# One transfer instead of four for a turned tile, the order made by the fetch, and sums of fetched tiles no longer forced

## The chip, the cores and the metric

The kernel runs on one core of a Trainium2 chip. A core has a matrix engine (TensorE, PE in the profile, its weight loads PEld), a vector engine (VectorE, DVE), a scalar engine (ScalarE, ACT), a general engine (GpSimd, POOL) and a sync engine (SyncE, SP) whose queue issues most transfers; 16 DMA engines carry the transfers. The metric is the time of one execution on the device in microseconds (us).

## The reference

Attention with a block mask over 4 batches of 8 heads, 768 positions and 64 columns; its output, laid out as 768 x 512 for each batch, goes through a Fourier mix and a two-layer channel network. All of it is float32.

```python
scores = scale * np.matmul(q, k.transpose(0, 1, 3, 2))        # (4, 8, 768, 768)
scores = np.where(mask, scores, -1000000000.0)                # blocks of 32 x 32
attn = np.exp(scores - max) ; attn = attn / (sum + 1e-09)
x = np.matmul(attn, v) -> (4, 768, 512)
mixed = np.real(fft(fft(x, axis=1), axis=2))
u = x + mixed
un = (u - mean(u)) / np.sqrt(var(u) + 1e-06)                  # over the 512 columns
out = u + np.maximum(un @ w_ch1, 0.0) @ w_ch2                 # 512 -> 2048 -> 512
```

## The kernel before

**Attention** goes in slots. A slot is two units; a unit is one chunk of 128 keys against 384 queries, for a pair of heads. There are 24 slots to a batch (6 for each of 4 pairs of heads), 96 in all. A slot multiplies the scores on PE (line 578), takes their exponential on ACT and multiplies the values in on PE (line 652), one or two slots later. The mask is applied in one of two ways. Early on PE adds it to the scores in two more products of a unit (line 588), ACT's exponential (line 598) writes the result, and sums of the weights are gathered by DVE (line 633) or POOL (line 638). Once `masks["by_pe"]` is false, ACT writes the exponential back (line 606) and DVE multiplies it with the mask (line 608). Pairs of heads from the sixth on are fetched in blocks of 32 x 32 (`load_blocks`, line 230): four transfers of 96 KB each for a tile of queries or keys (`qb`, `kb`), in pieces of 32 numbers, 128 bytes.

**The mixer** of a batch runs beside the attention of the next one. First its steps on x: folding, products with cosine and sine tables, normalising. Each step makes three tiles of 128 positions x 512 columns for each of two halves of the positions, `un`. The channel network wants them turned, columns on the partitions. For the last batch PE turns them. For batches 0, 1 and 2, which this change is about, the path is:

- `un_blocks` (line 1010): DVE turns each 32 x 32 block of a tile in place.
- Also in `un_blocks` (line 1013): SP writes the tile to a scratch tile `far` in memory. Four transfers, one for each 32 partitions, put every block where it belongs: `far` of a half is 32 x 16 x 384, and a piece is 32 numbers, 128 bytes.
- `un_back` (line 1022): SP fetches both halves into `unT`, four transfers of 32 partitions each for a half, 192 KB each. Every piece read is a row of 384 numbers.
- `right` (line 1053): four DVE sums of blocks of the fetched `unT`, which the first products of the channel network need (Strassen's scheme with seven products instead of eight, `quad`, line 1091). `left` (lines 1066, 1067, 1073) makes the same kind of sum from the weights.
- `quad` and `channels` (line 1147) then multiply; DVE adds the product to x (line 1150) and SP stores it (line 1158). Only when x of batch b - 2 is stored may `place` (ACT, line 676) write attention results of batch b into the same room.

**The order** is written out when the kernel is built, by a planner with a clock `when` for each engine and a cost for each step. Two lists hold the mixer's work: `apart`, the steps up to and including `right`, and `late`, the products. `gap` takes steps of `apart` where they fit beside PE's work; a step of kind "b", which all four sums are, has to wait in `gap` until the planner's clock has reached `state["back"]`, the time at which it expects the fetch to be in. The planner sets that in `un_back`, `BACK` after its own clock. Behind the four sums stands the step `go`: it makes `late` available and sets `masks["by_pe"]` to false. At the end of a slot of the third and fourth batch, where `late` is empty and few steps of `apart` are left, a loop takes up to four of them whatever the clock says:

```python
for _ in range(4 if phase > 1 and not late and len(apart) < 6 * T else 0):
    if apart and not late:
        do_apart()
```

The engines follow the order of the build: an instruction that waits holds up everything behind it on its engine, and so does a transfer in the queue of SP.

Of the kernel before, what the change touches and what calls it, by code (L numbers as in the profile page):

```python
# [11 lines left out]
FP32 = mybir.dt.float32  # L12
# [10 lines left out]
def _words(ap, n):  # L23

    return bass.DRamTensorHandle(ap.tensor.name, (2 * n,), I32)
# [74 lines left out]
def kernel(  # L100
# [14 lines left out]
    nc = tc.nc  # L115

    B, H, S, D = q.shape
    DM = H * D
    FF = w_ch1.shape[1]
    P = 128  # L120
    C = S // P
    BLK = 32
    NB = S // BLK
    NR = sampled_blocks.shape[1]
    HS = S // 2
# [4 lines left out]
    T = C // 2  # L130
# [54 lines left out]
    far_p = ctx.enter_context(tc.tile_pool(name="far_p", bufs=1, space=bass.MemoryType.DRAM))  # L185
# [7 lines left out]
    when = {"PE": 0.0, "ACT": 0.0, "DVE": 0.0, "POOL": 0.0}  # L193
# [106 lines left out]
    def bit(n):  # L300
# [5 lines left out]
                      in_=bass.AP(tensor=_words(sampled_blocks, NB * NR), offset=0,  # L306
                                  ap=[[0, NB], [1, 2 * NB * NR]]))
# [670 lines left out]
    def mixer(b, xA, xB):  # L978


        uns, unT = {}, {}
# [21 lines left out]
        lines = {}  # L1003

        def un_blocks(half, m):

            un = uns.pop((half, m))
            if half not in lines:
                lines[half] = far_p.tile([BLK, DM // BLK, HS], FP32, tag=f"un{half}", name="far")
            nc.vector.transpose(out=un, in_=un)  # L1010
            for g in range(P // BLK):
                n = m * P + g * BLK
                nc.sync.dma_start(out=lines[half][:, :, n:n + BLK],
                                  in_=un[BLK * g:BLK * g + BLK, :].rearrange(
                                      "j (t i) -> j t i", i=BLK))

        def un_back():

            for half in range(2):
                unT[half] = tr_p.tile([P, ND, T * P], FP32, tag="tr", name="unT")  # L1020
                for a in range(P // BLK):
                    nc.sync.dma_start(out=unT[half][BLK * a:BLK * a + BLK, :, :],
                                      in_=lines[half].rearrange(
                                          "j (k a) n -> a j k n", a=P // BLK)[a])
            state["back"] = max(when["PE"], state["ready"]) + BACK

        t, s = {}, {}
        K1, K2 = slice(0, ND // 2), slice(ND // 2, ND)
# [169 lines left out]
        def outputs(r, m, after):  # L1198
# [60 lines left out]
            if r == 1:  # L1259
# [5 lines left out]
              for h in range(2)]  # L1265

        ft = [[("d", lambda h=h, m=m: un_blocks(h, m), 0.0, 0.0, 0.7) for m in range(T)]
              for h in range(2)]

# [9 lines left out]
        if not last:  # L1279
            before = first + [pq[1], ar[0][1], ar[1][1], sp[0][1],  # L1280
                              pq[2], wh[0][1], ft[0][1], ar[0][2], ar[1][2], sp[0][2],
                              pq[0], wh[0][2], ft[0][2], ar[0][0], ar[1][0], sp[0][0],
                              sp[1][1], wh[0][0], ft[0][0], sp[1][2], wh[1][1], ft[1][1],
                              sp[1][0], wh[1][2], ft[1][2], wh[1][0], ft[1][0]]
            after = ([("-", un_back, 0.0, 0.0, 0.0)] + le +
                     [("b", lambda i=i: right(i, 0, 1, 2), 0.0, 0.0, 1.0) for i in (1, 2, 3, 4)])
# [5 lines left out]
        for r in range(0 if last else NF // 4):  # L1292
# [9 lines left out]
    MOST, LEAST = 9.6, 2.5  # L1302
    COVER = 100.0
    AHEAD = 2.2
    BACK = 9.0
    ALONE = 3.0
    LEAVES = 9.0
    SP = UP // SLOT
# [2 lines left out]
    short, apart, late, due = deque(), deque(), deque(), deque()  # L1311
    asked = set()
    needed = set()
    state = {"paired": False, "total": None, "w": 0, "got": 0, "owed": 0.0, "ready": 0.0,
             "back": 0.0}
# [9 lines left out]
    def do_apart():  # L1325
        kind, fn, pe, act, dve, _ = apart.popleft()
        if kind[0] in "dwb":
            dve += behind(kind)
            state["ready"] = busy("DVE", dve, {"w": rstd_at[0] if rstd_at else 0.0,
                                               "b": state["back"]}.get(kind, state["ready"])) + HOP  # L1330
            fn()
            return
        done = state["ready"]
        if kind != "-":
            at = bank(kind[0])
            done = busy("PE", pe, done) + HOP
        fn()
        if act:
            done = busy("ACT", act, done) + HOP
        if dve:  # L1340
            done = busy("DVE", dve, done) + HOP
        if kind != "-":
            give(at, done - HOP)
        state["ready"] = done
# [74 lines left out]
    def slot(sl):  # L1419
        phase, r = divmod(sl, SB)  # L1420
        n, s = divmod(sl, SP)
# [48 lines left out]
        if s >= (5 if reuse else 3) and (n, 0) in oT_at and once(n):  # L1470
            b, j = pairs[n]
# [13 lines left out]
        if sl < B * SB and n % NP == 1 and s == 1:  # L1485
            b = pairs[n - 1][0]
# [35 lines left out]
            gap(rest())  # L1522

        for _ in range(4 if phase > 1 and not late and len(apart) < 6 * T else 0):
            if apart and not late:
                do_apart()

        must = (3, 5) if paired else (2, 5)
# [5 lines left out]
        while short and (not more or soon) and (  # L1534
                s in must or len(short) > 1 or phase == 0 or soon or sl == B * SB):
            ready = [i for i in short if max(i[1], min(free[i[0]])) <= when["PE"] + 0.1]
# [36 lines left out]
    for sl in range(B * SB + 1):  # L1573
        slot(sl)
        if sl == B * SB - 4:
            flag = highest()
        if sl == B * SB - 2:
            over = nc.values_load(flag[0:1, 0:1], min_val=0, max_val=1)
# [107 lines left out]
```

## Time and profile before

| what | value |
|---|---|
| median of 3 runs | 1062.29 us (1061.61 to 1062.72) |
| the profiled execution, its own time | 1060.62 us |
| its span in the trace | 1058.8 us, granted clock 0.991 |
| PE busy | 1022.0 us, 97% |
| DVE, ACT, POOL busy | 677.8, 356.5, 241.6 us |
| transfers of `far` (72 of 64 KB) and of `unT` (24 of 192 KB) | SP queue |

The profile names engines as above; SPq, PEq and so on are the queues in front of them. A row of a timeline gives the start and the length in us, the engine, the line in the kernel, the operation, what it writes and reads, how many instructions are merged and, in brackets, how long the engine had been idle before and what ended that. A wait for several things is put down to the one that came last by the profile's reckoning; transfers on the same queue can be mistaken for each other there. A row of stretches gives for each engine the busy time (and the instructions), then the granted clock of PE, the mean busy share of the 16 DMA engines, and GB/s.

### The profile page before, as it was taken

To read this page: it belongs to the slowest core of one execution; us is meant where nothing else is said; L and a number is where in the kernel's file an instruction comes from. 1 tells how busy PE (TensorE), PEld (TensorE's weight loads), DVE (VectorE), ACT (ScalarE), POOL (GpSimd) and SP (SyncE) were. 2 spreads that over 40 slices of the span, in tenths; PEclk is the share of its full clock that TensorE was granted. 3 is DMA by queue.
4 is the path that set the end of the run, shared out by engine and by line. 5 is a ranking of instruction groups with operands and counts; after the bars stand their busy time and mean duration, and the time that the engine had idled before them with its cause. 6 is when DMAs were issued, how large, how long until landed. Compare 5 with 4: busy or idle time off the path is not lost.

```text
span 1058.8 us, 12480 instructions
## 1 busy us (share of the span) xinstructions
PE 1022.0 (97%) x4334; PEld 529.7 (50%) x4334; DVE 677.8 (64%) x1236; ACT 356.5 (34%) x718; POOL 241.6 (23%) x272
## 2 busy tenths in 40 slices
PE   8999999987999999999999999899999999999996
PEld 4333345433465554444444654344444654578575
DVE  6898795968754845564578466665457364674663
ACT  6988755553120112342441210253220211210210
POOL 1000183554200100554553001255520001000000
PEclk9999999998999999999999999999999999999999
DMA  7757422381000124222230003621000001000001
GB/s 214 230 170 225 108 46 46 50 147 28 1 0 11 20 44 96 57 38 44 41 56 1 1 11 60 134 43 27 12 10 5 1 1 37 24 1 1 1 16 47
DMA packets 162017, 55.72 MB, mean 53 GB/s; under 512 B 146572, under 2 KB 155034, under 8 KB 161946
## 3 DMA queue, kind: packets, MB, share of 16 engines
q1 hardware_dynamic: 160694, 54.11, 22.7%
q10 hardware_dynamic: 1220, 0.72, 0.3%
q8 instruction: 36, 0.59, 0.2%
q14 instruction: 35, 0.29, 0.1%
q0 software_dynamic: 32, 0.01, 0.0%
HBM read 41.44 MB, written 11.01 MB: 50 GB/s over the span
## 4 chain that ended last, share of the span: by engine, by line
PE 82%; DVE 6%; DMA 3%; ACT 3%; SPq 2%; issue 2%; POOL 0%; ACTq 0%; DVEq 0%
PE y L1147 22%; PE z L1091 15%; PE s L578 11%; PE o L652 9%; PE yp L1091 7%; PE yy L1212 7%; PE xp L1091 4%; PE zp L856 2%; PE sp L719 1%; DVE t L1053 1%; ACT e L598 1%; DMA kb<-in_k_dram 1%; PE s L588 1%; DMA out_dram<-x 1%; PE sp L733 1%
## 5 line engine op out<-in xcount | busy, mean ns | idle before, releaser
L638 POOL TENSOR_TENSOR acc<-acc,e 128x384 f32<-128x384 f32 x162 | 164.6, 1052 | 97.4 <-DVE e L608 81.1
L578 PE MATMUL s<-qT,kT 64*128 64x384 f32 x768 | 156.5, 523 | 20.4 <-DVE e L608 13.1
L652 PE MATMUL o<-e,vr 128*64 128x384 f32 x768 | 142.4, 498 | 0.0
L1147 PE MATMUL y<-w_sb,hB 128*128 128x512 f32 x288 | 128.6, 597 | 0.3 <-DVE x L1150 0.3
L1147 PE MATMUL y<-w_sb,hA 128*128 128x512 f32 x288 | 127.9, 595 | 0.0
L1150 DVE TENSOR_TENSOR x<-y,x 128x512 f32<-128x512 f32 x72 | 49.7, 691 | 111.7 <-PE y L1147 111.6
L608 DVE TENSOR_TENSOR e<-s,mask 128x768 f32<-128x768 f32 x92 | 83.8, 951 | 58.1 <-ACT s L606 49.9
L578 PEld LDWEIGHTS s<-qT,kT 64*128 64x128 f32 x768 | 64.4, 187 | 100.1 <-DVE e L608 28.0
L638 POOL TENSOR_TENSOR acc<-e 128x384 f32<-128x384 f32 x44 | 48.5, 1123 | 257.3 <-PE sp L733 127.2
L606 ACT ACTIVATE s<-s 128x768 f32<-128x768 f32 x92 | 70.0, 792 | 92.6 <-PE s L578 92.4
L1091 PE MATMUL z<-unT,t 128*128 128x384 f32 x256 | 93.2, 487 | 0.7 <-DVE hA L1096 0.7
L598 ACT ACTIVATE e<-s 128x768 f32<-128x768 f32 x100 | 76.0, 810 | 48.6 <-PE s L588 29.6
L1147 PEld LDWEIGHTS y<-w_sb,hB 128*128 128x128 f32 x288 | 53.6, 191 | 67.2 <-issue 65.7
L1147 PEld LDWEIGHTS y<-w_sb,hA 128*128 128x128 f32 x288 | 53.7, 190 | 63.7 <-issue 60.2
L652 PEld LDWEIGHTS o<-e,vr 128*64 128x64 f32 x768 | 48.1, 137 | 71.5 <-issue 68.0
L1096 DVE TENSOR_TENSOR hA<-z,hA 128x384 f32<-128x384 f32 x64 | 35.7, 557 | 68.5 <-PE z L1091 68.5
L1100 ACT ACTIVATE hA<-hA 128x384 f32<-128x384 f32 x64 | 33.4, 523 | 123.8 <-DVE hA L1096 123.8
L1091 PEld LDWEIGHTS z<-unT,t 128*128 128x128 f32 x256 | 48.5, 190 | 35.4 <-DVE hA L1096 2.0
L1100 ACT ACTIVATE hB<-hB 128x384 f32<-128x384 f32 x64 | 33.5, 523 | 86.2 <-DVE hB L1096 83.8
L1111 ACT COPY hA<-xp 128x384 f32<-128x384 f32 x32 | 15.3, 478 | 128.6 <-PE xp L1091 128.6
L1091 PE MATMUL yp<-unT,w_sb 128*128 128x384 f32 x128 | 46.7, 487 | 0.8 <-ACT hA L1111 0.6
L1091 PE MATMUL xp<-unT,w_sb 128*128 128x384 f32 x128 | 47.2, 492 | 0.0
(208 smaller groups left out, 1364.2 us busy)
## 6 DMA issues: line engine op xcount, KB each, us to landing
wraw<-in_moe_w_ch_dram SPq DMA_DIRECT2D x32, 512.0 KB
vr<-in_v_dram SPq DMA_DIRECT2D x30, 192.0 KB
far<-un SPq DMA_DIRECT2D x72, 64.0 KB
unT<-far SPq DMA_DIRECT2D x24, 192.0 KB
qb<-in_q_dram SPq DMA_DIRECT2D x44, 96.0 KB
kb<-in_k_dram SPq DMA_DIRECT2D x44, 96.0 KB
x<-oT SPq DMA_DIRECT2D x192, 12.0 KB
out_dram<-x SPq DMA_DIRECT2D x11, 252.0 KB
```

Of the source, the lines that this page charges most:

```text
L578: nc.tensor.matmul(s[:, i, 0:HS], kT[rows, c * P:(c + 1) * P], qT[rows, queries], start=True, stop=u not in by_pe)
L598: nc.scalar.activation(out=e, in_=s[:, :, 0:HS], func=ACT.Exp, scale=scale)
L606: nc.scalar.activation(out=s[:, :, 0:HS], in_=s[:, :, 0:HS], func=ACT.Exp, scale=scale)
L608: nc.vector.tensor_tensor(out=e, in0=s[:, :, 0:HS], in1=m.broadcast_to([P, 2, HS]), op=ALU.mult)
L638: nc.gpsimd.tensor_add(out=acc[:, i, :], in0=start[:, i, :], in1=e[:, i, :])
L652: nc.tensor.matmul(o[D * i:D * i + D, :], vt[:, i, c, :], e[:, i, :], start=(c == 0), stop=(c == C - 1))
L1091: nc.tensor.matmul(to, a[:, k, :], c[:, k, :], start=(k == 0), stop=(k == ND // 2 - 1))
L1096: tt(out=to, in0=ps, in1=a, op=ALU.add)
L1100: nc.scalar.activation(out=h, in_=h, func=ACT.Relu)
L1147: nc.tensor.matmul(y, hs[0, half][:, l, m * P:(m + 1) * P], w2_sb[:, 4 * r + l, :], start=(l == 0), stop=(l == 3))
L1150: nc.vector.tensor_tensor(out=x[:, m, :], in0=y, in1=x[:, m, :], op=ALU.add)
L1212: nc.tensor.matmul(ps, a[:, k, :], c[k // 2][:, k % 2, :] if isinstance(c, list) else c[:, k, :], start=(k == 0), stop=(k == 3))
```

## The change

It has three parts. The scratch tile `far` takes a turned tile as it is, 128 partitions of 512 numbers, in one transfer of 256 KB where there were four of 64 KB. The order is now made by the fetch: its eight transfers still fill 32 partitions each with 192 KB, but every piece they read is 32 numbers, 128 bytes, 1536 pieces to a transfer where there were 128. In the planner, `BACK` goes from 9.0 to 13.0 for the first batch and 12.0 for the others, and the loop at the end of a slot no longer takes a sum of fetched tiles before the planner's clock has come to `state["back"]`.

```diff
             if half not in lines:
-                lines[half] = far_p.tile([BLK, DM // BLK, HS], FP32, tag=f"un{half}", name="far")
+                lines[half] = far_p.tile([T, P, DM], FP32, tag=f"un{half}", name="far")
             nc.vector.transpose(out=un, in_=un)
-            for g in range(P // BLK):
-                n = m * P + g * BLK
-                nc.sync.dma_start(out=lines[half][:, :, n:n + BLK],
-                                  in_=un[BLK * g:BLK * g + BLK, :].rearrange(
-                                      "j (t i) -> j t i", i=BLK))
+            nc.sync.dma_start(out=lines[half][m], in_=un)
 
         def un_back():
             for half in range(2):
                 unT[half] = tr_p.tile([P, ND, T * P], FP32, tag="tr", name="unT")
+                of = lines[half].rearrange("m (g j) (k a i) -> a j k (m g) i",
+                                           j=BLK, a=P // BLK, i=BLK)
                 for a in range(P // BLK):
-                    nc.sync.dma_start(out=unT[half][BLK * a:BLK * a + BLK, :, :],
-                                      in_=lines[half].rearrange(
-                                          "j (k a) n -> a j k n", a=P // BLK)[a])
-            state["back"] = max(when["PE"], state["ready"]) + BACK
+                    nc.sync.dma_start(
+                        out=unT[half][BLK * a:BLK * a + BLK].rearrange(
+                            "j k (g i) -> j k g i", i=BLK),
+                        in_=of[a])
+            state["back"] = max(when["PE"], state["ready"]) + BACK[b > 0]
...
-    BACK = 9.0
+    BACK = 13.0, 12.0
...
         for _ in range(4 if phase > 1 and not late and len(apart) < 6 * T else 0):
-            if apart and not late:
+            if apart and not late and (apart[0][0] != "b" or
+                                       state["back"] < max(when["DVE"], when["PE"]) + 0.2):
                 do_apart()
```

## The prediction

> **What bounds the kernel now.** I read the head of the page first, then PE's waits, then the timelines of the three places where `unT` is fetched.
>
> ```profile
> span 1058.8 us, 12480 instructions
> PE 1022.0 (97%) x4334; PEld 529.7 (50%) x4334; DVE 677.8 (64%) x1236; ACT 356.5 (34%) x718; POOL 241.6 (23%) x272
> PE 82%; DVE 6%; DMA 3%; ACT 3%; SPq 2%; issue 2%; POOL 0%; ACTq 0%; DVEq 0%
> ```
>
> PE bounds it. Only 36.8 us of the span (1058.8 - 1022.0) are free of a product, so a change that adds and removes no product can gain only there, or where PE ran at a lower clock. PE's waits, in total, times and longest:
>
> ```profile
> PE s L578 <- DVE e L608: 13.1, 4, 8.1
> PE s L578 <- ACT e L598: 6.9, 12, 1.9
> ```
>
> The largest is a score product waiting for DVE's masking, and most of that is one wait of 8.1 us. The timeline at the first fetch shows it:
>
> ```profile
> 222.52 0.68 DVE L1010 STREAM_TRANSPOSE un<-un 128x512 f32<-128x512 f32 x1
> 223.78 2.69 SPq L1013 DMA_DIRECT2D far<-un  x4
> 226.16 0.95 DVE L633 TENSOR_TENSOR acc<-acc,e 128x768 f32<-128x768 f32 x1
> 226.32 1.56 PE L578 MATMUL s<-qT,kT 64*128 64x384 f32 x8
> 226.51 5.19 SPq L1022 DMA_DIRECT2D unT<-far  x8
> 229.58 1.56 PE L578 MATMUL s<-qT,kT 64*128 64x384 f32 x8
> 234.24 1.56 PE L578 MATMUL s<-qT,kT 64*128 64x384 f32 x8
> 236.96 1.11 DVE L1053 TENSOR_TENSOR t<-unT 128x768 f32<-128x768 f32 x1 [9.85 <-DMA kb<-in_k_dram]
> 241.33 1.74 DVE L1053 TENSOR_TENSOR t<-unT,t 128x768 f32<-128x768 f32 x1
> 244.33 1.80 DVE L608 TENSOR_TENSOR e<-s,mask 128x768 f32<-128x768 f32 x2
> 245.32 2.93 PE L578 MATMUL s<-qT,kT 64*128 64x384 f32 x8 [8.08 <-DVE e L608]
> ```
>
> The four forced sums stand on DVE right behind the row of 226.16. DVE stands still 9.85 us until the fetch is in (the release is booked on `kb`, which follows on the same queue), sums until 243, and only then reaches the masking that PE waits for. PE loses 8.08 us, and the first eight products after it take 2.93 us where the same take 1.56.
>
> At the second fetch nothing is lost:
>
> ```profile
> 394.15 8.93 SPq L1022 DMA_DIRECT2D unT<-far  x8
> 404.00:414.00 10.00, 10.00 (x24) 4.35 (x24) 5.63 (x7) 0.00 (x0) 0.00 (x0) 1.00 0.47 110
> 408.08 0.95 DVE L1053 TENSOR_TENSOR t<-unT 128x768 f32<-128x768 f32 x1
> 410.90 0.69 DVE L1150 TENSOR_TENSOR x<-y,x 128x512 f32<-128x512 f32 x1
> ```
>
> The sums start without a wait and PE is busy 10.00 of 10 us. At the third, two things go wrong one after the other:
>
> ```profile
> 649.41 5.02 SPq L1013 DMA_DIRECT2D far<-un  x4
> 653.53 0.69 DVE L1150 TENSOR_TENSOR x<-y,x 128x512 f32<-128x512 f32 x1 [0.75 <-PE y L1147]
> 656.34 2.63 SPq L1013 DMA_DIRECT2D far<-un  x4
> 659.07 1.21 SPq L1158 DMA_DIRECT2D out_dram<-x  x2
> 662.31 0.48 ACT L676 COPY x<-xt 128x384 f32<-128x384 f32 x1 [17.97 <-DMA out_dram<-x]
> 664.54 2.79 PE L578 MATMUL s<-qT,kT 64*128 64x384 f32 x8 [3.06 <-DVE e L608]
> 667.26 4.12 PE L1147 MATMUL y<-w_sb,hB 128*128 128x512 f32 x8
> 676.03 1.82 DVE L1053 TENSOR_TENSOR t<-unT 128x768 f32<-128x768 f32 x1 [3.93 <-DMA kb<-in_k_dram]
> 680.78 0.68 DVE L1150 TENSOR_TENSOR x<-y,x 128x512 f32<-128x512 f32 x1
> ```
>
> The last x of half A is ready at 654.2 (653.53 + 0.69), but its store is issued at 659.07, behind eight writes of `far`. ACT waits for the store until 662.31; its exponential, DVE's masking and PE's scores follow, and PE loses 3.06 us. Then the sums wait 3.93 us on DVE, and the last sum into x stands behind three of them (680.78).
>
> **The change, part by part.** *One write instead of four.* The counts and sizes, what two kinds of transfer get out of the DMA engines, and what products of line 1147 take undisturbed:
>
> ```profile
> L1013 SPq DMA_DIRECT2D far<-un x72: 549/627/2036, 193.0 to 665.1; - x72
> unT<-far SPq DMA_DIRECT2D x24, 192.0 KB
> qb<-in_q_dram SPq DMA_DIRECT2D x44, 96.0 KB
> 230.00:231.00 1.00, 1.00 (x10) 0.51 (x8) 0.00 (x0) 0.87 (x3) 1.00 (x2) 1.00 1.08 218
> 247.00:248.00 1.00, 1.00 (x4) 0.10 (x2) 0.09 (x1) 0.80 (x1) 1.00 (x2) 0.50 0.99 160
> 331.06 10.30 PE y L1147 x24
> ```
>
> 54 issues of 0.627 us fall away, 34 us of SP's queue over the kernel. SP bounds nothing by itself, so this counts in one place. At 649 to 659 six of the eight issues ahead of the store go: 3.8 us (6 x 0.627), and the store moves from 659.07 to about 655.3. That is more than PE's 3.06 us, so I take them as gone, and with them the slow products behind: 1.2 us (2.79 - 1.56) and 0.7 us (4.12 less 3.4, a third of 10.30). Sum at the third fetch 5.0 us. The bounds are 0, if the write of 256 KB keeps the store back instead, and 5.0.
>
> The Trainium skill, DMA: Bandwidth & Descriptors, section Issuing engines are not separate DMA queues, says that a sequencer's issue time is usually small beside the transfer. By that, joining issues would save next to nothing and the 5.0 us would not come. The rows are against it here: eight issues of `far` stand in the queue between 649.41 and 659.07, and the store behind them. I go by the rows, and keep the page's case as a rival below.
>
> *The fetch makes the order.* Still 24 fetches of 192 KB, but in pieces of 128 bytes. No row shows that fetch. Its nearest row is the load of `qb` at 247, the same direction and the same pieces: 160 GB/s with the engines full (0.99). The old fetch of long rows ran at 218 (row of 230). Eight transfers are 1573 KB: 7.2 us before, 9.8 us now, 2.6 us more. Lower bound 7.2 us, upper bound 15.0 us, if reading such pieces back from scratch goes only as fast as the queue wrote them (64 KB in 0.627 us, 105 GB/s). I take 9.8. In return the last write before the fetch holds SP 0.6 us instead of 2.69, and the transpose before it ends at 223.2, so the fetch starts at about 224.0 instead of 226.51, 2.5 us sooner. The two nearly cancel: it lands at about 237, as now. The next load of `kb` stands behind it on the queue as it does now.
>
> The Trainium skill, DMA: Bandwidth & Descriptors, section Specifications, gives 512 bytes as the least transfer for full rate. The rule speaks against the change, and the two rows agree with it in kind (160 against 218 GB/s). Where it would lead if the loss were far greater is the third rival.
>
> *Sums not forced, expected later.* At the first fetch the planner now expects the data 13 us after the last transposed tile, on the trace's time at 223.2 + 13 = 236.2. The loop no longer takes the sums at the end of the slot of 226 (229.6), nor can they go at the end of the next (234.2). They go in the slot that begins at 234.24, two slots later. By then the data is all but there: 237 less 236.2 leaves DVE a wait of up to 1 us instead of 9.85. Behind the sums on DVE is queued the masking of the slot after. Four sums at the present 1.1 to 1.7 us end at 242 to 243, and the scores of that slot's successor have to wait for a masking behind them. PE is dry there from about 240.8 (two slots of 3.26 us, 226.32 to 229.58, after 234.24), so I leave 2 us of wait. What goes: 8.08 us and 1.4 us (2.93 - 1.56) of slow products, 9.5 in all. What comes: the 2 us, and two more slots masked by PE, because `go` stands behind the sums.
>
> ```profile
> 224.62 0.33 PE s L588 x4
> ```
>
> Those are 0.33 us a slot in the chain, 0.7 us. Sum at the first fetch: 9.5 - 2.0 - 0.7 = 6.8 us gained; bounds 3 (the sums end at 246, as long as PE's dry spell lasts) and 9.
>
> At the second fetch the planner's 12 us put the sums one product of 3.4 us later, behind the row of 410.90. Work that hides it: PE's products until 414. The second half of the fetch takes 1.3 us longer (half of 2.6) and has 3.4 us to do so. Zero; if the cover were gone, up to 3 us lost. At the third the sums likewise fall behind the last product of batch 1, so the last sum into x goes ahead of them and its store starts up to 5 us sooner than behind 680.78, and the next use of that room with it. PE's leftovers there:
>
> ```profile
> 676.00:680.00 4.00, 2.97 (x9) 1.31 (x8) 3.93 (x3) 0.48 (x1) 2.71 (x3) 1.00 0.40 93
> 692.00:696.00 4.00, 3.32 (x18) 1.26 (x20) 2.95 (x4) 3.21 (x10) 3.23 (x4) 1.00 0.33 53
> ```
>
> 1.0 and 0.7 us are idle. I count 1.0 us of the 1.7 as gained; the bounds are -2 (the first products of batch 2 wait for sums that start later) and +1.7.
>
> Sum: 6.8 + 5.0 + 0 + 1.0 = 12.8 us. For waits that the new order brings and that I can't place I take 1.5 us off: 11.3. The profiled execution took 1060.62 us (span 1058.8 and 1.8 around it), 0.16% under the median of 1062.29, so it would come to 1049.3, and the median to 1051.0.
>
> **The rivals.**
> *Only the first fetch gains.* The store at 659 is held by the data of the writes, not by their issue, or another wait takes its place. For it: the second issue row, 5.02 us for four, is longer than four times 0.627. Against: the chain goes through SP's issues there. Gain 6.8 - 1.5, about 5.3 us: 1057.0.
>
> *The sums stall again.* The fetch takes the 15.0 us of the upper bound and lands 5.2 us after my 237; the sums hold DVE until 248, and the first fetch gains nothing. The third keeps its 5.0 us, as it has time: 1057.3 by the median. For it: the scratch rows are read in scattered pieces; against: `qb` is too, at 160 GB/s.
>
> *The fetch is far slower, and it ends slower than before.* If the pieces come back at 65 GB/s, a fetch takes 24.2 us and lands at 251. The sums then end at 257, the scores two slots on start at 258.5 instead of about 249.7 (245.32 + 2.93 + 1.4): 9 us lost. At the second fetch the second half alone takes 12.1 us from about 402 and the sums wait 3; at the third they start at 685, 9 us later than now, with the first products of batch 2 behind. Together 21 us lost less the 5.0 us of the store: 1078. It decides from about 85 GB/s downwards, half of what `qb` shows. The skill's 512-byte rule, which points this way, would have to bite twice as hard as in the row.
>
> *The change does nothing that counts*: the loop finds the sums due at the same slot after all, and the gain by the store is eaten by the longer fetch: 1062. Against: 13 us after 223.2 is past the end of both slots.
>
> **How the numbers follow.** Forecast 1051.0: 0.58. Only the first fetch: 0.14. Stall again: 0.10. Far slower, or a new order that costs more than it saves: 0.12. Nothing: 0.06, half of it within 0.2%, which is about what a measurement of this kernel can tell from no change. Faster 0.84, same 0.03, slower 0.13. The forecast's own range is 1045 to 1055: all bounds good (9 + 5.0 + 1.7, 1046.6, and no new waits) to a first fetch at its lower bound of 3 us (1054.8). The range of 1045 to 1062 takes in the next two rivals and no change at all, and leaves 0.05 below and 0.13 above.
>
> **What would show it.** Right: no idle of DVE over 2 us ahead of the first sum at any fetch; the sums at the first fetch after 236; PE's longest wait on the masking under 3 us; in the slot of 234 the row of line 588 still there; ACT's copy at 662 gone to about 658 with PE's 3.06 us; 18 writes of `far`; a fetch in about 10 us. Wrong: a bracket of some microseconds on the first sum again; a store of x still landing after 661; the engines full at well under 160 GB/s while `unT` comes in; PE's clock low in a new place.

## The result, and the profile after

| | us |
|---|---|
| kernel before, median of 15 runs beside it | 1061.33 (1059.89 to 1064.09) |
| changed kernel, median of 15 runs | 1058.52 (1054.26 to 1059.52) |
| ratio | 0.9966, interval 0.9957 to 0.9975 |
| predicted, by the 1062.29 of then | 1051.0 |

The change makes the kernel faster, by 2.8 us where 11.3 were predicted. The profiled execution took 1059.17 us, 0.65 over the median. It is 1.45 us under the profiled execution of the kernel before (1060.62), where the medians are 2.8 apart: the two profiles show only half of the difference. Its page begins:

```profile
span 1057.5 us, 12421 instructions
...
PE 1022.8 (97%) x4338; PEld 530.7 (50%) x4338; DVE 675.3 (64%) x1235; ACT 356.2 (34%) x718; POOL 240.2 (23%) x270
```

PE's waits (total, times, longest):

```profile
PE s L578 <- DVE e L608: 6.5, 3, 3.7
...
PE z L1090 <- DVE e L608: 3.4, 1, 3.4
...
PE z L1090 <- DVE hA L1095: 2.0, 1, 2.0
PE z L1090 <- DVE t L1052: 1.6, 1, 1.6
```

The wait of 8.1 us on the masking is gone. In its place stand 3.7 and 2.0 us on the masking (the first row) and the 3.4, 2.0 and 1.6 us of the others. (Line numbers of the changed kernel are one or two lower than before: the write is line 1011, the fetch 1020, the sums 1052, the quad 1090, the product of `channels` 1146, the add to x 1149, the store 1157.)

The best ruler is the start of a quad's first product, the row `xp<-unT,w_sb`, since each quad follows a fetch and its sums. Between two such marks the order of PE's work is nearly the same in both kernels:

| mark | before, starts at | after, starts at | gained since the mark above | foreseen |
|---|---|---|---|---|
| last quad ahead of the second fetch | 391.37 | 386.73 | +4.6 (first fetch) | +6.8 |
| first quad of batch 1 | 428.22 | 427.48 | -3.9 (second fetch) | 0 |
| last quad of batch 1 | 634.00 | 633.25 | 0.0 | 0 |
| first quad of batch 2 | 675.63 | 670.10 | +4.8 (the store) | +5.0 |
| second quad of batch 2 | 700.41 | 698.75 | -3.9 (after the third fetch) | +1.0 |
| end of the span | 1058.8 | 1057.5 | -0.4 | 0 |

Beside these the prediction took 1.5 us off for waits that it couldn't place. Nearly all that the first fetch and the store gain is given back at two places, a few microseconds further on.

Of the first +4.6, only 2.9 come at the fetch itself. By the slot of 206 us (206.48 before, 206.24 after) the changed kernel is 0.2 ahead; 1.5 more come between there and the fetch, where a wait of PE of the kernel before is gone:

```profile
223.01 1.62 PE L578 MATMUL s<-qT,kT 64*128 64x384 f32 x8 [1.23 <-ACT e L598]
```

This wait stands in the three kernels with the old writes and in none of the ten with the new layout; why it goes stays open. From the slot behind it (226.32 before, 224.59 after) to the mark it is 165.05 us before and 162.14 after. The profiled executions differ by up to 2.2 us already at 87 us (86.52 to 88.75), long before the first of these transfers, so what the first fetch gains is best counted from this slot.

The same by stretches between the marks (length, PE's busy time and products, granted clock, DMA share, GB/s), of the kernel before:

```profile
391.37:428.22 36.85, 36.85 (x120) 1.00 0.37 84
634.00:675.63 41.63, 38.57 (x121) 0.96 0.49 92
675.63:700.41 24.78, 22.25 (x96) 1.00 0.35 77
```

and of the changed one:

```profile
386.73:427.48 40.75, 38.79 (x121) 0.96 0.52 73
633.25:670.10 36.85, 36.85 (x121) 1.00 0.67 99
670.10:698.75 28.65, 23.36 (x97) 0.94 0.35 72
```

The second stretch of the changed kernel has no idle PE left: the third fetch's store does what was foreseen. In the first and the third PE stands idle for 2.0 and 5.3 us (0 and 2.5 before), and full clock is lost besides.

**At the first fetch**, in the timeline of the changed kernel:

```profile
222.90 0.34 SPq L1011 DMA_DIRECT2D far<-un  x1
...
223.28 10.23 SPq L1020 DMA_DIRECT2D unT<-far  x8
...
237.96 1.31 DVE L1052 TENSOR_TENSOR t<-unT 128x768 f32<-128x768 f32 x1 [4.02 <-issue]
...
239.08 1.46 PE L1090 MATMUL xp<-unT,w_sb 128*128 128x384 f32 x4
...
244.19 1.81 DVE L608 TENSOR_TENSOR e<-s,mask 128x768 f32<-128x768 f32 x2
...
245.19 1.61 PE L1090 MATMUL z<-t,w_sb 128*128 128x384 f32 x4 [3.36 <-DVE e L608]
...
246.40 4.43 DVE L761 TENSOR_TENSOR x<-x,r 128x512 f32<-128x512 f32 x5
...
250.75 0.55 DVE L1095 TENSOR_TENSOR hA<-z,hA 128x384 f32<-128x384 f32 x1
...
251.35 1.56 PE L1090 MATMUL z<-unT,t 128*128 128x384 f32 x4 [1.99 <-DVE hA L1095]
```

One write of 0.34 us, and the fetch at 223.28. Its eight issues hold SP for 10.23 us, and the first sum starts at 237.96, so the data are in at about 238 where 237 was foreseen. But DVE has reached the sums at 233.94 (237.96 less 4.02) and stands 4.02 us, and the quad follows at once: PE runs its first products from 239.08 and then waits 3.36 us for the quad's third product, the first `z`, and 1.99 us more for a later one. Neither wait ends with a sum of fetched tiles. The first `z` reads the second sum, which is done at 240.93 (239.30 and 1.63 us). It starts at 245.19, when the first masking behind the four sums has ended (244.19 and 0.94 us): in the kernel a `z` and the scores share two rooms in PSUM, the memory that PE writes its products into, and a room is free only when its scores are masked. The later `z` waits for an add into hA (line 1095, 250.75), which stands on DVE behind 4.43 us of scaling (line 761). The wait has moved from the scores into the quad.

**At the second:**

```profile
395.76 10.46 PE L1146 MATMUL y<-w_sb,hA 128*128 128x512 f32 x24
...
406.06 0.49 PE L675 MATMUL xt<-ident,oT 128*128 128x128 f32 x3
406.26 0.69 DVE L1149 TENSOR_TENSOR x<-y,x 128x512 f32<-128x512 f32 x1 [2.74 <-PE y L1146]
...
410.51 0.48 ACT L676 COPY x<-xt 128x384 f32<-128x384 f32 x1 [13.10 <-DMA out_dram<-x]
...
412.73 2.35 PE L578 MATMUL s<-qT,kT 64*128 64x384 f32 x8 [1.96 <-DVE e L608]
```

And before:

```profile
410.70 3.60 PE L1147 MATMUL y<-w_sb,hB 128*128 128x512 f32 x8
...
415.03 0.48 ACT L676 COPY x<-xt 128x384 f32<-128x384 f32 x1 [12.98 <-DVE x L1150]
```

In the changed kernel PE turns the attention's result (line 675) after three products of line 1146, and ACT may copy it into x only when the store of the third x, ready at 406.95, has landed: 410.51. Before, a fourth product (3.60 us, at 410.70) stood between the two, and the copy, at 415.03, waited for no store. Exponential, masking and scores stand behind the copy.

**At the third,** on SP's queue and then on the engines:

```profile
653.50 1.17 SPq L1157 DMA_DIRECT2D out_dram<-x  x2
...
657.40 10.23 SPq L1020 DMA_DIRECT2D unT<-far  x8
667.74 2.29 SPq L1157 DMA_DIRECT2D out_dram<-x  x3
670.41 6.60 SPq L230 DMA_DIRECT2D kb<-in_k_dram  x4
677.11 2.87 SPq L1157 DMA_DIRECT2D out_dram<-x  x6
```

```profile
657.76 0.48 ACT L676 COPY x<-xt 128x384 f32<-128x384 f32 x1 [14.16 <-DMA far<-un]
...
670.30 0.69 DVE L1149 TENSOR_TENSOR x<-y,x 128x512 f32<-128x512 f32 x1 [3.02 <-PE y L1146]
...
687.09 0.48 ACT L676 COPY x<-xt 128x384 f32<-128x384 f32 x1 [4.82 <-DMA out_dram<-x]
...
689.37 2.50 PE L578 MATMUL s<-qT,kT 64*128 64x384 f32 x8 [3.71 <-DVE e L608]
```

The store of half A's last x is issued at 653.50 instead of 659.07, the copy goes at 657.76 instead of 662.31, and PE's 3.06 us are gone. Then the fetch takes SP until 667.6. The stores behind it follow at 667.74, the load of keys holds SP for 6.60 us more, and the last x, ready at 671.0 (670.30 + 0.69), is stored only from 677.11. ACT's next copy into that room stands 4.82 us until 687, and PE 3.71 us.

### The profile page after: what moved, and what is told of

The parts are those of the page before. It is cut to its first block, busy times and chain, and to the rows that moved or that the text cites. A ratio compares the mean times of both kernels' runs of the same rounds, so it can differ in the third digit from the quotient of the medians.

```text
span 1057.5 us, 12421 instructions
## 1 busy us (share of the span) xinstructions
PE 1022.8 (97%) x4338; PEld 530.7 (50%) x4338; DVE 675.3 (64%) x1235; ACT 356.2 (34%) x718; POOL 240.2 (23%) x270
## 4 chain that ended last, share of the span: by engine, by line
PE 82%; DVE 8%; ACT 3%; DMA 3%; issue 2%; SPq 1%; ACTq 0%; DVEq 0%
PE y L1146 23%; PE z L1090 15%; PE s L578 10%; PE o L652 9%; PE yp L1090 7%; PE yy L1211 7%; PE xp L1090 4%; PE zp L856 2%; ACT e L598 1%; DMA out_dram<-x 1%; PE sp L719 1%; PE s L588 1%; DVE t L1052 1%; DVE x L926 1%; DVE acc L633 1%
## 5 line engine op out<-in xcount | busy, mean ns | idle before, releaser
L1090 PE MATMUL z<-t,w_sb 128*128 128x384 f32 x128 | 46.9, 489 | 5.0 <-DVE e L608 3.4
L1090 PE MATMUL z<-t,t 128*128 128x384 f32 x128 | 47.8, 497 | 0.0
```

What stands on the lines that cost most here:

```text
L1090: nc.tensor.matmul(to, a[:, k, :], c[:, k, :], start=(k == 0), stop=(k == ND // 2 - 1))
```

## The experiments

Ratios are to runs of the kernel before on the same chip, whose medians were 1061.8 to 1062.1 us. The changed kernel itself stands at 0.9966.

**The two parts by themselves.** Transfers alone: the changed kernel with the planner of before.

```diff
-    BACK = 13.0, 12.0
+    BACK = 9.0, 9.0
...
-            if apart and not late and (apart[0][0] != "b" or
-                                       state["back"] < max(when["DVE"], when["PE"]) + 0.2):
+            if apart and not late:
```

> The one write and the reordering fetch alone, planner as before. Theory A (planner decides at the first two fetches, transfers at the third): the first sum waits some 10 us on DVE again and PE 8 to 9 us, no wait at the second fetch, PE's 3.06 us at the third gone; about 4 us under before, 1057. Rival B (the fetch in small pieces, which holds SP's queue about 10 us, makes stores late at the second and third fetch): PE waits 2 us at the second fetch here too, and the time is 1060 or more.

Measured 1058.39 us, ratio 0.9958 (0.9944 to 0.9971). The marks: 391.46 (nothing gained), 428.31, 634.13, 670.98 (4.7 gained over the kernel before), 698.54 (2.8 of it given back). At the first fetch DVE waits 12.06 us for the data and PE 8.66 us. So the gain of the transfers is the store's at the third fetch, and the loss behind it is theirs too. The transfers alone already take the time of the whole change (1058.52).

Planner alone: the kernel before with the two edits of the planner.

> The planner's two edits alone, transfers as before. Theory A: the first fetch gains 4 to 5 us, the second loses some 3 us (PE waits 2 us for a masking behind a late store, then a low clock), the third keeps the 3.06 us of before; 1059 to 1061. Rival B: no loss at the second fetch, 1056 to 1057.

Measured 1061.28 us, ratio 0.9991 (0.9982 to 1.0): nothing that can be told from no change. The marks: 389.32 (2.05 gained) and 428.10 (1.9 of it given back). This execution is 1.05 us behind the kernel before already at the slot of 206 (207.53 and 206.48), so the first fetch itself gains 3.1. The loss at the second fetch is the planner's.

**The third fetch.** First, what do the small pieces cost? The changed kernel, whose fetch reads rows of 512 numbers and leaves the order as it is:

```diff
                     nc.sync.dma_start(
-                        out=unT[half][BLK * a:BLK * a + BLK].rearrange(
-                            "j k (g i) -> j k g i", i=BLK),
-                        in_=of[a])
+                        out=unT[half][BLK * a:BLK * a + BLK].rearrange(
+                            "j k n -> j (k n)").rearrange("j (m d) -> j m d", m=T),
+                        in_=lines[half][:, BLK * a:BLK * a + BLK, :].rearrange("m j d -> j m d"))
```

> The changed kernel with the fetch reading rows of 512 numbers, without making the order (so the channel network gets the columns of the normalised tiles in the wrong order): what the small pieces cost. SP's eight issues should fall from 10.2 to about 5 us and the fetch land 2.5 to 3 us earlier. Theory A: the first fetch gains up to 2.6 us, second unchanged (its wait comes from the order), third up to 1.6 us: 1055 to 1057. Rival B: the waits at the second and third fetch go altogether, 1051 to 1053.

Measured 1053.27 us, ratio 0.9914 (0.99 to 0.9927): 5 us less than the changed kernel. The eight issues hold SP 3.71 us instead of 10.23, and the queue behind them is early enough:

```profile
657.30 3.71 SPq L1018 DMA_DIRECT2D unT<-far  x8
...
663.09 8.35 SPq L230 DMA_DIRECT2D kb<-in_k_dram  x4
671.54 2.90 SPq L1155 DMA_DIRECT2D out_dram<-x  x6
...
681.86 0.46 ACT L676 COPY x<-xt 128x384 f32<-128x384 f32 x1
```

The copy stands for nothing, no score waits behind it, and the second quad of batch 2 starts 22.7 us after the first (692.80 less 670.07) instead of 28.65. Of the 5 us nearly all is here. At the second fetch a score still waits 1.82 us, so the waits of the third go, as rival B has it, and that of the second stays, as theory A has it.

Is it the place in SP's queue, or the data and the DMA engines? The changed kernel, with one load of keys behind the last store instead of ahead of it:

```diff
-        if s == 0 and 0 < n < len(pairs) - 1:
+        if s == 0 and 0 < n < len(pairs) - 1 and n != 13:
             load_k(n + 1)
...
                 until(lambda: (b - 2, 1) in finished)
+                if n == 13:
+                    load_k(n + 1)
```

> The changed kernel, with the load of one tile of keys (four transfers of kb, which stood on SP from 670.41 to 677.0) issued behind the last store of batch 1's x instead of ahead of it. Theory A (at the third fetch SP's queue is the limit: the fetch of small pieces holds it 10.2 us, the stores and the load stand behind it, and the last store lands so late that ACT waits 4.82 us and PE 3.71 us): the last store is issued at about 671 and lands at about 680, both waits go, the second quad of batch 2 starts at 694.5 to 696 instead of 698.75, and the time is 1054.5 to 1056.5. Theory B (the DMA engines or the data of the store are the limit, not the place in the queue): the store still lands at 686 to 687, the quad stays at 698.5, and the time at 1058 to 1059.

Measured 1053.39 us, ratio 0.9919 (0.9905 to 0.9933). The fetch still holds SP 10.12 us, until 667.6, and the stores no longer stand behind the load:

```profile
667.71 7.21 SPq L1157 DMA_DIRECT2D out_dram<-x  x9
676.67 6.28 SPq L230 DMA_DIRECT2D kb<-in_k_dram  x4
...
683.03 0.48 ACT L676 COPY x<-xt 128x384 f32<-128x384 f32 x1 [0.65 <-DMA kb<-in_k_dram]
```

The stretch from the first to the second quad of batch 2 takes 23.0 us (670.21 to 693.22), 5.65 less than in the changed kernel. It is the place in the queue, as theory A has it.

Does the gain ahead of it come from the number of writes, or from their longer rows? The changed kernel with four writes for each tile again, to the same places:

```diff
-            nc.sync.dma_start(out=lines[half][m], in_=un)
+            for g in range(P // BLK):
+                gs = slice(BLK * g, BLK * g + BLK)
+                nc.sync.dma_start(out=lines[half][m, gs], in_=un[gs, :])
```

> The changed kernel, with each turned tile written in four transfers of 32 partitions again, to the same places in the new layout of the scratch tile (rows of 2 KB); fetch and planner are those of the changed kernel. Theory A (the gain at the third fetch came from the number of issues ahead of the store on SP): the issues take 0.4 to 0.6 us each, the store of half A's last x goes 2 to 4 us later than 653.50, ACT's copy at 657.76 comes 2 to 4 us later and PE loses 2 to 4 us there; the time is 2 to 5 us over the changed kernel, 1060.5 to 1063.5. Theory B (it came from the layout, rows of 2 KB instead of pieces of 128 bytes, however many transfers there are): the store stays within 1 us of 653.5, and the time within 1 us of the changed kernel's 1058.5.

Measured 1063.24 us, ratio 1.0011 (1.0001 to 1.0021), 4.7 us over the changed kernel, in the bounds of theory A. An issue of a quarter takes 0.42 us where it took 0.627 with pieces of 128 bytes, so both the number and the rows count. The way is only partly theory A's. In its profile the third fetch has lost 1.7 us of its 4.8 (38.56 us from 637.42 to 675.98, against 36.85), with a score waiting 1.43 us again, below the 2 to 4 us expected. The last x of half A is ready at 657.64 and its store is issued at 660.89, 3.25 us later (4.85 before, 0.03 in the changed kernel), but 2.7 us of that are a wait of SP's queue that the profile books on an earlier store, and not issue time. At the first fetch, from the slot ahead of it to the mark, 1.8 us are lost (163.98 against 162.14). Some 2.1 us of the distance between the two profiled executions (1065.71 and 1059.17) were there at 87 us, before the first write, and say nothing of the writes.

**The second fetch.** The first try went by the sums: `BACK` of 9.0 for this fetch alone, as before (13.0 and 12.0 for the others).

> The changed kernel with 9 us instead of 12 for the second fetch alone. Theory A: the fourth sum and the step behind it fit ahead of the slot again, one more product goes ahead of it, PE's 2 us there go with the low clock behind; about 3 us under the changed kernel, 1055.5. Rival B: the wait stays, 1058.5.

Measured 1059.3 us, ratio 0.9973 (0.9961 to 0.9985), the same as the changed kernel, as rival B has it. The sums do go earlier (403.65), and still only three products stand ahead of the copy:

```profile
410.46 0.48 ACT L676 COPY x<-xt 128x384 f32<-128x384 f32 x1 [13.54 <-PE o L652]
...
412.69 1.78 PE L578 MATMUL s<-qT,kT 64*128 64x384 f32 x8 [2.41 <-DVE e L608]
```

So it isn't the sums as such. What differs from the kernel before is the number of products that the planner puts between the last add into half A and the placing. It takes one more when `owed`, PE's time that a slot owes to the products, is at least half a product, 1.725 us by the planner's own arithmetic. These are numbers of the planner as it writes the order, not of a trace: in the kernel before `owed` stood at 1.752 there; in the changed kernel, whose `go` comes later, at 0.927; in this run at 1.725, on the threshold to three digits, and no product was taken. So the direct test: the changed kernel with one product more at that place.

```diff
                 until(lambda: (b - 2, 0) in finished)
+                if b == 2:
+                    channel_step()
```

> The changed kernel, with one product of line 1146 more ahead of the second fetch's placing of results into x of batch 0; nothing else is moved up to there. Theory A (the changed kernel places one product too early, before the store of x has landed, and so loses at the second fetch what it gained at the first): ACT's wait for the store at 410 shrinks by about 3.4 us, PE's 1.96 us behind it goes, the first quad of batch 1 starts at 424 to 425.5 instead of 427.48, and the time is 2 to 3.5 us under the changed kernel, 1055 to 1056.5. Theory B (the loss at the second fetch is the later sums, or data that come at a fixed time, and the place of the product doesn't matter): the quad stays within 0.5 us of 427.5 and the time within 0.7 us of the changed kernel's 1058.5.

Measured 1056.57 us, ratio 0.9941 (0.9927 to 0.9955), 2.0 us under the changed kernel and at the small end of theory A. The loss at this place is gone:

```profile
409.14 3.60 PE L1146 MATMUL y<-w_sb,hB 128*128 128x512 f32 x8
...
413.71 0.48 ACT L676 COPY x<-xt 128x384 f32<-128x384 f32 x1 [13.21 <-DMA out_dram<-x]
...
417.21 1.56 PE L578 MATMUL s<-qT,kT 64*128 64x384 f32 x8
```

36.85 us from mark to mark (389.81 to 426.66), to the hundredth what it took before. The quad itself starts later than the 424 to 425.5 expected, as the profiled run had lost 3.1 us at the first fetch, in the same order of work: see the last section. That run is the slowest of the six (1058.98 us). Why the median gains 2.0 us where the stretch gains 3.9 isn't shown.

**The first fetch.** Does the landing set what is left there? The changed kernel, with half 0 of the first batch fetched as soon as its third tile is written:

```diff
             nc.sync.dma_start(out=lines[half][m], in_=un)
+            if (half, m) == (0, 0) and b in (0,):
+                fetch(0)
...
             for half in range(2):
+                if half not in unT:
+                    fetch(half)
```

> The changed kernel, in the same order on PE, DVE and ACT, with the first batch's half 0 fetched as soon as its third tile is written (about 211.7 instead of 223.3). Theory A (the landing of the first fetch at 238 sets the rest of the loss there): half 1 lands at 229 to 231, DVE's 4.02 us ahead of the first sum goes, the sums begin at 234 and PE's waits of 3.36 and 1.99 us in the first quad shrink to under 2 us together; the first quad starts at about 239 as now, and the next milestone, q8, 3 to 4 us before 386.73. The second fetch takes 0 to 1 us of it back, as the store of x is then just as late against the products. Time 1054.5 to 1057. Theory B (order on DVE, not landing): q8 within 1 us of 386.7, time 1058 to 1059. Theory C (five us of fetch on SP ahead of the later tiles delay their writes and the queries' loads by as much): half 1 still lands after 234 and less than half of the gain comes.

Measured 1057.8 us, ratio 0.9962 (0.9947 to 0.9976), not to be told from the changed kernel. Theory C came about: SP is held 5.40 us by the early half from 214.53, the writes and the queries' load behind it are late, half 1 can only be fetched from 229.33, and the sums start at 237.62. Counted from the slot ahead of the fetch (225.75 here, 224.59 without the edit) that is 1.5 us earlier: DVE waits 2.52 us instead of 4.02, PE in the quad 1.52 and 3.31 us, and the mark is 1.8 us nearer. That leans to A, but the landing of 229 to 231 was not reached and the time is the same, so this run doesn't decide between A and B.

The next one moves the sums instead: `BACK` of 17.0 for the first batch and 9.0 for the second, which also puts two products ahead of the second placing.

```diff
-    BACK = 13.0, 12.0
+    BACK = 17.0, 9.0, 12.0, 9.0
...
-            state["back"] = max(when["PE"], state["ready"]) + BACK[b > 0]
+            state["back"] = max(when["PE"], state["ready"]) + BACK[b]
```

> The changed kernel, with 17.0 us in place of 13.0 for the first batch and 9.0 for the second: the first sums go one slot later and two products of line 1146 stand ahead of the second placing. For the first fetch, theory A (what is left there is the late landing at 238, and DVE's 4.02 us behind it): the sums start without a wait at 238.5 to 240, PE's waits of 3.36 and 1.99 us in the first quad shrink under 2 us together, and the first quad of batch 2's attention, q8, starts 2 to 4 us before 386.73. Theory B (the quad's own products follow the sums at once wherever these stand, and DVE has sums, masking and scaling to do ahead of them): PE waits 4 us or more in the first quad again and q8 is within 1 us of 386.7. For the second, by theory A of the run with one more product, no loss between q8 and the first quad of batch 1 against the kernel before (36.85 us there): the quad starts at q8 + 37. Time by both theories A: 1052 to 1054.5; by A at the second alone: 1055 to 1056.5; by neither: 1058.5.

Measured 1049.09 us, ratio 0.9876 (0.9861 to 0.989):

```profile
239.17 0.95 DVE L1052 TENSOR_TENSOR t<-unT 128x768 f32<-128x768 f32 x1
...
245.78 1.56 PE L1090 MATMUL xp<-unT,w_sb 128*128 128x384 f32 x4
...
248.46 1.45 PE L1090 MATMUL z<-t,w_sb 128*128 128x384 f32 x4
...
251.04 1.45 PE L1090 MATMUL z<-unT,t 128*128 128x384 f32 x4
...
679.69 2.93 PE L578 MATMUL s<-qT,kT 64*128 64x384 f32 x8 [3.54 <-DVE e L608]
```

The sums start at 239.17 with no wait, PE has another slot of attention ahead of the quad, and no product of the quad waits. The mark of 386.73 is at 382.12, 9.25 us ahead of the kernel before. From the slot ahead of the fetch (225.16) it is 156.96 us, 8.1 less than the 165.05 before, about the bracket of 8.08 us; the rest comes ahead of the fetch. At the second fetch nothing waits (35.5 us from mark to mark). Both theories A hold, and the time is below their 1052 to 1054.5. The third fetch keeps its wait (679.69).

**Together.** The last order and the load of keys behind the store:

> The two edits that helped put together: 17.0, 9.0 and 12.0 us for the three fetches, and the load of keys behind the last store at the third. Theory A (the losses at the first, second and third fetch are separate and add up): the run with 17.0 and 9.0 took 1049.1 us and still shows PE's wait of 3.54 us and slow products at 679.69; these go, the second quad of batch 2 starts 23 us after the first instead of 29.4, and the time is 1043 to 1045.5. Rival (the load of keys, now after the fetch's tail, lands too late in this order, or another store is late): the second quad starts 26 us or more after the first and the time is 1047 to 1049.5.

Measured 1044.37 us, ratio 0.9831 (0.9817 to 0.9844), the fastest of all: 14.2 us under the changed kernel and 17.4 under the one before. The two edits by themselves took 9.4 and 5.1 us off, 14.6 together: the losses are separate and add up. In PE's timeline of it no row at the first or second fetch has a bracket, and at the third the one of 1.59 us ahead of a `z` is left.

And what are the new transfers worth once the order is right? The transfers of before in the order of the run with 17.0:

> The kernel before's transfers (four writes, the fetch of long rows) in the order of the run with 17.0, 9.0 and 12.0, which took 1049.1 us. Theory A (the first fetch is settled by the order alone, as its data come at 237 to 238 with either kind of transfer; only the third fetch needs the new write): q8 is within 1.5 us of 382.1, the second fetch loses nothing, ACT's copy at the third is late by 3 to 5 us and PE waits about 3 us there, but the second quad of batch 2 doesn't wait for a store behind the fetch; the time is 1049 to 1053. Theory B (the order only pays with the new transfers): q8 at 385 or later, the time over 1055.

Measured 1051.74 us, ratio 0.9904 (0.9889 to 0.992), 2.65 us more than with the new transfers. The first mark is at 382.91, 0.8 us from that of the new ones, and from the slot ahead of the fetch (225.95) it takes 156.96 us, to the hundredth what it takes with the new transfers: the first fetch is settled by the order alone. At the third ACT's copy waits for the store and PE 3.04 us, while the second quad of batch 2 follows the first in 24.2 us: the store's gain and the loss behind the fetch, traded one for the other.

## Why the prediction was right or wrong

*Right.* The sign. The write: 18 issues of 0.34 us, and the fetch with them earlier. The third fetch's store: 5.0 taken, 4.8 found, by the chain that the prediction named; with four writes again 1.7 of it goes, and with the old transfers in a better order PE waits 3.04 us there as before. In the slot that stood at 234 before and starts at 232.51 now, the products of line 588 are there, as foreseen; only one slot more is masked by PE, not two.

*Right by luck: the landing.* At 238 where 237 was. From the first issue to the first sum the fetch takes 14.7 us; the 10.45 of before and the 2.6 foreseen make 13.05. It also begins 0.7 us sooner than foreseen (223.28, not 224.0), and the two errors nearly cancel. The 10.23 us for which its issues hold SP is another number than the 9.8 us of data at 160 GB/s, though they lie close.

The Trainium skill, DMA: Bandwidth & Descriptors, section Issuing engines are not separate DMA queues, has issue time as usually small beside the transfer. For the one write the runs agree: 0.34 us for 256 KB. For the fetch of small pieces they are against it: its issues hold SP for 10.23 of those 14.7 us.

*Wrong: the first fetch, 6.8 foreseen, 4.6 found, and only 2.9 of it there.* The step that failed is "I leave 2 us of wait". That PE would wait for a masking behind the four sums was right, but its size was not: the prediction's own figures give some 3 us (sums until 243, 0.9 us of masking, PE dry from 240.8), and 3.36 came. And it wasn't the only wait: the quad follows the sums at once, and its adds stand on DVE behind 4.43 us of scaling, which costs PE 1.99 us more. Together 5.35 us where 2 were taken. Of the 4.02 us that DVE stood, up to 1 us was foreseen: DVE came to the sums at 233.94, before the 236.2 at which the planner counted the data in. A slot later (17.0 in place of 13.0) both of PE's waits go, and the same stretch gains 8.1 us. The 1.5 us ahead of the fetch weren't foreseen at all.

*Wrong: the second fetch, 0 foreseen, -3.9 found.* The prediction looked for the cover of the sums and found it, rightly: the sums start without a wait at 406.87. But it took the order around them as fixed. With the later `go` the planner's `owed` is below a threshold (0.927 against 1.725), one product of 3.4 us falls behind the placing, and the copy meets a store that hasn't landed. The run with one more product shows this, and the planner alone gives back 1.9 of its 2.05 us there.

*Wrong: after the third fetch, +1.0 foreseen, -3.9 found.* The prediction noted that the fetch would take 2.6 us longer and asked only when its data would be in. It left out what its own rows give beside the start: how long the issues hold SP's queue. Eight issues of 10.23 us in place of 5.19 hold what SP has behind them, and there stand three stores, a load of 6.60 us and the store that ACT waits for. The sentence that "its store starts up to 5 us sooner" fell short on that: the last x was ready at 671.0 instead of 681.5 and the quad started 5.5 us sooner, but the row of stores that holds it began at 677.11 instead of 680.41, 3.3 us sooner. Long rows and the moved load each give the 5 us back.

The 1.5 us for waits that can't be placed were the right thought and a fifth of the size: 3.9 and 3.9 us came. The forecast's own range of 1045 to 1055 misses the time by 3.5 us; only the wide one, up to 1062, which takes in no change at all, holds it. Of the rivals the first two give nearly the right time (1057.0 and 1057.3), but by other ways: the first has the store not coming sooner at all, and that part came; the second has the sums stall until 248 with nothing gained at the first fetch.

## What to carry to other kernels

A transfer costs its queue as well as its landing: ask what stands behind its issues, not only when its data are in, and put a store that frees a room ahead of a load that has time. When a planner's due time is changed, follow the order to the next two or three places where it chooses, since a threshold there can put one product on the other side of a wait. A sum that is late costs nothing if another slot of work stands ahead of what waits behind it; moved so that its reader follows at once, it only moves the wait.

## What was not expected of the hardware

**A fetch in small pieces holds the issuing queue.** Issues of the same 192 KB (shortest, median and longest, in ns):

```profile
L1020 SPq DMA_DIRECT2D unT<-far x24: 557/1274/1650, 223.3 to 666.0; - x24
```

with pieces of 128 bytes, and with rows of 2 KB, in the run with long rows:

```profile
L1018 SPq DMA_DIRECT2D unT<-far x24: 303/428/471, 224.5 to 660.6; - x24
```

A factor of three. In the stretch 660 to 670 the DMA share is 1.60 at 134 GB/s with small pieces, and 0.77 at 162 GB/s with long rows: the engines are busy twice as much for fewer bytes. (A share over 1 means that packets overlap in time on an engine; in the second stretch loads of keys in small pieces run too.)

**The price of a wait on PE is not its length.** After the waits in the first quad the granted clock falls to about a half for some microseconds, and how much of the work that follows falls into it differs from run to run, in the same order. In the changed kernel the products behind the second wait took 1.56 and 1.45 us; in the run with one more product:

```profile
251.50 2.93 PE L1090 MATMUL z<-unT,t 128*128 128x384 f32 x4 [3.31 <-DVE hA L1095]
254.22 2.77 PE L1090 MATMUL yp<-t,w_sb 128*128 128x384 f32 x4
```

The next quad starts 3.1 us later than in the changed kernel: 1.5 us of that is longer waits (3.52 and 3.31 us against 3.36 and 1.99), and the rest are slow products. In the stretch of 252 to 256 the granted clock is 0.50. The changed kernel spreads over 5.3 us (1054.26 to 1059.52, 15 runs) and the run with one more product over 5.8 (six runs), the fastest kernel, without these waits, over 1.9 (five runs). That the waits make the spread is not shown: the run with long rows waits 4.68 us in the first quad and spreads over 1.5 (five runs). The Trainium skill, TensorE: Matmul & The Clock Gate, Part 1: The HAM clock gate, tells of a clock gate that goes by free-running windows of 3.4 us of activity, and of counts of slow products that vary from run to run; the rows agree in kind.

**DVE's sums take 0.95 us or 1.75.** The same 128x768 sum takes 0.95 us at the second fetch, and 0.95 to 1.06 at the first in the run of the transfers alone; in the changed kernel's first fetch three of four take 1.63 to 1.75 us, while POOL sums `acc` (line 638) from 233.62 to 243.45. In the run of the transfers alone POOL has ended its sums at 238.79, and in the run with one more product it ends them at 242.74: there the last of the four, from 243.48, takes 0.95 us again. The Trainium skill, SBUF — State Buffer, section Terms, tells of a port pair that the two engines share, where one blocks the other for a whole instruction. The rows fit that, but it was seen and not tested by itself.
